# Second mixture of experts: raw float32 weights for few-token experts, splitting in an expert's own first tile, a ring of 21 raw pieces

## The chip, the cores and the metric

The kernel runs on one core of a Trainium2 chip. The metric is device microseconds of one execution. Three runs of the kernel before the change gave 1115.76, 1119.74 and 1121.19 us; their median is the time before.

The core's engines are TensorE (PE in the rows, its weight loads PEld), VectorE (DVE), ScalarE (ACT), GpSimd (POOL) and SyncE (SP). Each has its own instruction stream and takes it in order. SP issues nearly all plain DMAs here, POOL the indirect ones (gathers and scatters of rows by token number).

## The reference

Attention (4 x 8 heads, 576 positions, 64 wide, with rotary embedding) gives 2304 tokens of 512 numbers. A first mixture, in fact a dense gated layer with 1536 hidden columns, gives x. The change is in what follows:

```python
skip_score = x @ w_skip
do_compute = skip_score > 0
out = x.copy()
xc = x[do_compute]
e_idx = np.argmax(xc @ w_gate, axis=1)          # one of 8 experts
gate_w = softmax(xc @ w_gate)[its expert]
for e in range(8):
    h = np.maximum(xc[mask] @ w1[e], 0.0)       # 512 x 1024
    y[mask] = gate_w[mask, None] * (h @ w2[e])  # 1024 x 512
out[do_compute] = xc + y
```

With the inputs of the measurement the reference sends 299, 35, 55, 544, 28, 14, 322 and 1 tokens to experts 0 to 7.

## The kernel before

All matrix products are to be as exact as float32, but the fast operand type (float32r) isn't. So an operand a is split into a high part (a copy that ScalarE rounds to float32r) and a low part (a minus the high part, on VectorE or GpSimd), and a product is the sum of three: high x high, high x low, low x high.

**Order of the work.** Attention comes first (class `Attention`), then the first mixture (`Moe1`, chunks of 384 tokens, 12 steps f each), then the routing and the second mixture (`Moe2`). The code gives the order of each engine's instructions by hand; nothing is rescheduled. While the last chunk of the first mixture runs, `before(f)` loads and splits expert 0's weights into slots that are already free, then the first pieces of expert 1's. `first()` runs expert 0's first tile between the steps of the last chunk's routing: transposes and logits on PE, then `route` (L716 to L734, a chain of small VectorE operations), `place`, and the lists of the next tiles. Expert 0's first list is padded to 128 places there (`close_first`: before the last chunk it had 100 tokens), so that its count becomes 327.

**Experts and tiles.** `run` (L1259) takes expert after expert, in tiles of 128 tokens. Whether a tile exists is known only on the chip: `If` branches on every engine (L1291 for an expert's first tile, `more`, L1301 and L1327, for the later ones). A tile of more than 64 tokens goes through `ffn`: `up` (L1077, L1080: for each half of the 1024 columns 8 + 4 products of 512 columns), `turn` (L1134, transposes of h), `down` (L1150 to L1153: 24 products), `store` (L1158, L1159). A tile of at most 64 tokens (`few=True`) has the high and the low part of x side by side in one operand of 128 columns: 16 products up (L1094), a fold with the transpose (L1107), 16 products down (L1118).

**Weights before.** An expert has 8 raw pieces of 512 KB: 4 of w1, 4 of w2. `w_load` (L997) brings a piece into a ring of 7; `w_split` (L1015, L1017 high parts; L1020 low parts) splits it into one of two sets of slots, in turn for odd and even experts. An expert's first tile splits the next expert's weights (`work`, L1247): ScalarE, VectorE and GpSimd share that by the table `SPLITS`. Between the two halves of `turn`, `mid` transposes the next tiles' rows (`x_T`, L1063 to L1065), which POOL gathered (L1056). Each split piece's place in the ring is reloaded behind it in SP's stream.

**Lists.** After the routing, 8 lists of token numbers (L1043, 9 KB each, 12 bytes a place) are read from the table in DRAM, and VectorE limits the numbers (`numbers`, L1048) before POOL gathers the rows.

The lines on which the order rests:

```python
for e in range(E):
    if e == 0:
        self.more(0, n[0], ix[0], self.x01, self.x02, 1); continue
    ...
    with self.tc.If(n[e] > FEW) as cmp:                                   # L1291
        self.ffn(e, x0[e], self.work(e + 1, False), lambda: mid(False))
        self.more(e, n[e], ix[e], x1[e], x2, 1)
    with cmp.Else():
        self.ffn(e, x0[e], self.work(e + 1, True), lambda: mid(True), few=True)
```

Of the kernel before, what the change touches and what calls it, by code (L numbers as in the profile page):

```python
# [13 lines left out]
P = 128  # L14
# [8 lines left out]
class Attention:  # L23
    """Attention of all head pairs, one 128-row block of scores ("unit") after another; what
    a pair needs is prepared while the units before it run."""
# [45 lines left out]
    # the slots of it, from the pair's first unit  # L71
# [3 lines left out]
    # other slots for the first pair's, which all wait for, and the second's  # L75
# [47 lines left out]
    # the engines of RoPE and of the split: GpSimd (p), VectorE (v), ScalarE (a); of the first  # L123
    # pairs others
# [4 lines left out]
    # of the first pair's transposes and swaps, those that VectorE brings from PSUM  # L129
# [168 lines left out]
    def misc(self):  # L298
        """A bank for the slot's small transposes."""
# [42 lines left out]
    def sums(self, u):  # L342
        """1 / (row sums + 1e-9) of the pair."""
# [6 lines left out]
    def sums_out(self, u):  # L350
        """They leave as rows."""
# [13 lines left out]
    # a pair's thirds of halves, in the slots from LAG["pv"] after its first: early in a slot and late  # L365
# [67 lines left out]
class Weights:  # L433
    """Split weights live in slots of [128, 4, 512]; raw pieces of [128, 512] pass through a ring."""
# [14 lines left out]
    def slot(self, i, name):  # L449
        pool = self.early if i < self.nearly else self.late  # L450
        return pool.tile([P, 4, 512], F32R, tag=f"w{i}", name=name)

    def load(self, key, src, wide):
        """A piece in float32, or in float64 as pairs of words."""
# [5 lines left out]
    def narrow(self, key, hi, lo):  # L460
        """float64's words to float32: sign, exponent and fraction move into place; what is
# [953 lines left out]
```

## Time and profile before

| | us |
|---|---|
| median of three runs | 1119.74 |
| lowest, highest run | 1115.76, 1121.19 |
| span of the profiled execution, first to last instruction | 1110.7 |
| the same, from the first tile of expert 0 after the routing (862.5) to the end | 248.2 |

PE is busy for 987.0 us (89% of the span), VectorE 622.4, GpSimd 528.5, ScalarE 509.9. The mean granted TensorE clock is 0.964 of full speed. 121.2 MB are moved, 109 GB/s over the span. The profiled execution has no run time of its own beside its span; the span lies 9.0 us under the median of the runs.

How to read it: the busy shares are means over three stages with different limits. The page's 40 slices show PE at nine tenths or more through the first mixture, and holes in the last quarter only, which is where the changed code stands. What the change is worth is therefore read from a table of stretches of that quarter, from the waits of PE in it, and from the queue of DMAs.

### The profile page before, as it was taken

To read this page: it belongs to the slowest core of one execution; us is meant where nothing else is said; L and a number is where in the kernel's file an instruction comes from. 1 tells how busy PE (TensorE), PEld (TensorE's weight loads), DVE (VectorE), ACT (ScalarE), POOL (GpSimd) and SP (SyncE) were. 2 spreads that over 40 slices of the span, in tenths; PEclk is the share of its full clock that TensorE was granted. 3 is DMA by queue.
4 is the path that set the end of the run, shared out by engine and by line. 5 is a ranking of instruction groups with operands and counts; after the bars stand their busy time and mean duration, and the time that the engine had idled before them with its cause. 6 is when DMAs were issued, how large, how long until landed. Compare 5 with 4: busy or idle time off the path is not lost. (4 is left out here: it accounts for less than half of the span.)

```text
span 1110.7 us, 16633 instructions
## 1 busy us (share of the span) xinstructions
PE 987.0 (89%) x5883; PEld 834.7 (75%) x5883; DVE 622.4 (56%) x1006; ACT 509.9 (46%) x1093; POOL 528.5 (48%) x493
## 2 busy tenths in 40 slices
PE   5989889989997989899999999999998948996874
PEld 4766666666775878799999999999996736775763
DVE  6766776676774888863452432332546227615940
ACT  4777777776784333333432312322434226314510
POOL 6666678767821444452134152151345228514840
PEclk9999999999999999999999999999999968998896
DMA  5344455555423333332221212113245538704710
GB/s 160 101 117 107 121 153 132 140 148 127 124 78 129 114 114 103 108 86 85 58 71 56 60 29 71 44 29 98 73 125 166 160 99 270 236 31 141 250 46 3
DMA packets 81738, 121.20 MB, mean 109 GB/s; under 512 B 36645, under 2 KB 47541, under 8 KB 81600
## 3 DMA queue, kind: packets, MB, share of 16 engines
q1 hardware_dynamic: 77856, 110.02, 34.6%
q0 software_dynamic: 3744, 9.50, 2.7%
q8 instruction: 68, 1.11, 0.5%
q14 instruction: 70, 0.57, 0.2%
HBM read 88.78 MB, written 22.61 MB: 100 GB/s over the span
## 5 line engine op out<-in xcount | busy, mean ns | idle before, releaser
L614 POOL TENSOR_TENSOR hl<-h,hh 128x384 fp32r<-128x384 f32 x72 | 78.1, 1085 | 242.4 <-ACT hh L613 236.2
L252 DVE TENSOR_REDUCE nm<-S 128x1 f32<-128x576 f32 x144 | 108.5, 754 | 46.8 <-PE S L240 45.7
L260 ACT ACTIVATE P<-S,nm 128x576 f32<-128x576 f32 x144 | 107.0, 743 | 4.2 <-DVE nm L252 4.0
L1020 POOL TENSOR_TENSOR el<-we,eh 128x512 fp32r<-128x512 f32 (+1 forms) x55 | 85.0, 1571 | 42.4 <-ACT eh L1015 14.5
L613 ACT CAST hh<-h 128x384 fp32r<-128x384 f32 x72 | 37.0, 514 | 145.0 <-DVE h L612 145.0
L611 DVE TENSOR_TENSOR h<-g,h 128x384 f32<-128x384 f32 x72 | 40.0, 556 | 107.1 <-ACT h L610 107.1
L1020 DVE TENSOR_TENSOR el<-we,eh 128x512 fp32r<-128x512 f32 (+1 forms) x59 | 71.8, 1250 | 44.8 <-ACT eh L1015 38.6
L627 PE MATMUL Y<-ohi,hh 128*128 128x512 f32 x216 | 87.8, 407 | 5.4 <-ACT ohi L493 5.4
L270 PE MATMUL T<-ident,P 128*128 128x128 f32 x576 | 89.3, 278 | 0.0
L627 PE MATMUL Y<-ohi,hl 128*128 128x512 f32 x216 | 86.9, 402 | 1.4 <-POOL hl L614 1.3
L627 PE MATMUL Y<-olo,hh 128*128 128x512 f32 x216 | 86.0, 398 | 0.6 <-POOL olo L496 0.6
L319 PE MATMUL pv<-pt,rawv 128*64 128x384 f32 (+1 forms) x512 | 84.8, 432 | 1.5 <-ACT pt L285 1.4
L240 PE MATMUL S<-Ak,Aq 128*128 128x288 f32 x256 | 81.4, 333 | 1.5 <-ACT P L260 1.5
L604 PE MATMUL g<-xa,ghi 128*128 128x384 f32 x216 | 75.5, 350 | 7.1 <-DVE h L611 6.5
L240 PE MATMUL S<-Bk,Aq 128*128 128x288 f32 x256 | 73.1, 300 | 1.5 <-DMA Bk<-Ak 1.3
L610 ACT ACTIVATE h<-g 128x384 f32<-128x384 f32 x72 | 35.1, 487 | 85.4 <-PE g L606 81.6
L1015 ACT CAST eh<-we 128x512 fp32r<-128x512 f32 (+1 forms) x104 | 59.8, 649 | 30.9 <-DMA we<-in_moe_w_dram 16.6
L606 PE MATMUL g<-xa,glo 128*128 128x384 f32 x216 | 72.4, 335 | 0.0
L606 PE MATMUL v<-xa,vlo 128*128 128x384 f32 x216 | 72.2, 334 | 0.0
L604 PE MATMUL v<-xa,vhi 128*128 128x384 f32 x216 | 72.1, 334 | 0.0
L612 DVE TENSOR_TENSOR h<-v,h 128x384 f32<-128x384 f32 x72 | 40.2, 558 | 46.1 <-PE v L606 43.5
L270 PEld LDWEIGHTS T<-ident,P 128*128 128x128 f32 x576 | 63.5, 142 | 2.1 <-issue 1.2
(251 smaller groups left out, 2708.4 us busy)
## 6 DMA issues: line engine op xcount, KB each, us to landing
we<-in_moe_w_dram SPq DMA_DIRECT2D x64, 512.0 KB
xT<-x SPq DMA_DIRECT2D x32, 288.0 KB
x<-xT SPq DMA_DIRECT2D x24, 384.0 KB
Bk<-Ak SPq DMA_DIRECT2D x30, 288.0 KB
raw<-in_moe_w_gate_dram SPq DMA_DIRECT2D x12, 512.0 KB
raw<-in_moe_w_val_dram SPq DMA_DIRECT2D x12, 512.0 KB
raw<-in_moe_w_out_dram SPq DMA_DIRECT2D x12, 512.0 KB
rawk<-in_k_dram SPq DMA_DIRECT2D x16, 288.0 KB
```

Of the source, the lines that this page charges most:

```text
L240: nc.tensor.matmul(ps[:, c, :288], l, r[:, c * 288:(c + 1) * 288], start=(j == 0), stop=(j == len(ops) - 1))
L252: nc.vector.tensor_reduce(nm, st_u["S"], axis=AX.XY, op=ALU.max, negate=True)
L260: nc.scalar.activation(pt.rearrange("p (a b) -> p a b", a=2), st_u["S"], AF.Exp, bias=st_u["nm"], scale=1.0, accum_out=self.pairs[p]["l"][ ...
L270: nc.tensor.transpose(ps[:, kt * P:(kt + 1) * P], pt[:, kt * P:(kt + 1) * P], self.ident)
L319: nc.tensor.matmul(ps[a * D:a * D + D, :n], st["raw"]["v"][:, h, 2 * third + a], self.pt[:, 2 * third + a, c0:c0 + n], start=(third == 0), ...
L604: nc.tensor.matmul(ps[m], wh[:, kt, cols], xh, start=(kt == 0), stop=False)
L606: nc.tensor.matmul(ps[m], wl[:, kt, cols], xh, start=False, stop=(kt == KT - 1))
L612: nc.vector.tensor_tensor(h, ps["v"], h, op=ALU.mult)
L614: nc.gpsimd.tensor_tensor(hl, h, f32(hh), op=ALU.subtract)
L627: nc.tensor.matmul(self.acc[c][t], a[:, cols], b, start=(f == 0 and i == 0), stop=(f == FT - 1 and i == 2))
L1015: self.nc.scalar.copy(hi[:, cols], raw[:, cols])
L1020: eng.tensor_tensor(lo[:, cols], raw[:, cols], f32(hi[:, cols]), op=ALU.subtract)
```

## The change

- Experts with at most 64 tokens no longer use split weights. `raw_ffn` multiplies the unsplit float32 pieces by an unsplit float32 copy of the transposed rows (`xf`, written in `x_T` with one more ScalarE copy). Its products have 64 output rows; alternate ones go to the upper and the lower 64 rows of one PSUM bank, and a fold with `fold2` adds the two.
- Larger experts split their own weights, in their first tile, into one single set of slots (`homes`): high halves all on ScalarE, low halves all on VectorE (`half`). GpSimd splits nothing in this stage, and the next expert's weights are no longer touched (`work`, `SPLITS` are gone).
- Raw pieces stand in a ring of 21 (16 in the slots that the second set of split weights and the first mixture had, 4 in the old ring, 1 new). Experts 1 and 2 are loaded in `before` and `first`, 5 pieces of expert 3 at the start of `run`, the rest behind each expert, in SP's stream after its branch.
- The last tile of an expert, if it has at most 64 tokens, is found by arithmetic (`rest`): its list is read by a DMA of its own, at an address from a register, its numbers limited, its rows gathered. Of a larger expert these three stand ahead of the first tile, its transpose at that tile's end. The `Else` branches for few tokens in `more` go away.
- Expert 0's later tiles get a branch of their own; its second tile there transposes the third one's rows.

```diff
     def before(self, f):
-        if 4 <= f < 11:
-            for i in ((0,), (1,), (2, 3), (4,), (5, 6), (7,), (8, 9))[f - 4]:
+        if 4 <= f < 10:
+            for i in ((0,), (1,), (2, 3), (4,), (5, 6), (7,))[f - 4]:
                 self.w_splits(i, i + 1, "vv" if f > 8 else "vp")
+        if f in (8, 9):
+            self.raw_slots(2 * f - 16, 2 * f - 14)
+            for i in range(4):
+                self.w_load(1, 4 * f - 32 + i)
...
     def first(self):
+        self.raw_slots(4, 8)
+        for i in range(8):
+            self.w_load(2, i)
-        h0 = self.up(0, self.x00, 0, between={0: y_T[:2], 1: y_T[2:], 2: [(self.w_splits, 10, 12, "pp")], 3: lg[:1]})
+        h0 = self.up(0, self.x00, 0, between={0: y_T[:2], 1: y_T[2:], 3: lg[:1]})
-        self.w_splits(12, 14, "pp")
-        self.w_splits(14, 15, "vv")
-        self.w_splits(15, 16, "vv")
...
+    def half(self, e, i, k):
+        which, n = i // KT, i % KT // 2
+        hi, lo = (x[:, 2 * (i % 2) + k, :] for x in self.homes(which)[n])
+        raw = self.w.raw[e, i][:, k * 512:(k + 1) * 512]
+        self.nc.scalar.copy(hi, raw)
+        self.nc.vector.tensor_tensor(lo, raw, f32(hi), op=ALU.subtract)
...
+    def ffn(self, x, mid=None, few=False, split=None, end=None):
+        half(range(KT), 0)
+        half(range(KT), 1)
+        h0 = up(0, x, 0)
+        rows(range(0, 3))
+        h1 = up(0, x, 1)
+        turn(0, h0)
+        rows(range(3, 5))
         if mid:
             mid()
+        turn(1, h1)
+        rows(range(5, 8))
+        if end:
+            end()
+        down(0)
         store(x)
+    def raw_ffn(self, e, x, mid):
+        side = lambda ps, a: ps[a * FEW:(a + 1) * FEW]
+        for fh in range(2):
+            ps = self.bank("H", f"rH{fh}")
+            for kt in range(KT):
+                nc.tensor.matmul(side(ps, kt % 2), x["f"][:, kt * FEW:(kt + 1) * FEW],
+                                 self.w.raw[e, kt][:, fh * 512:(fh + 1) * 512],
+                                 start=(kt < 2), stop=(kt >= 2), skip_group_check=True)
+            nc.scalar.copy(h, ps)
+        mid()
+        for fh in range(2):
+            for i in range(4):
+                nc.tensor.matmul(ps[:, i * FEW:(i + 1) * FEW], hs[fh][:, i * P:(i + 1) * P], self.fold2, start=True, stop=True)
+            nc.scalar.activation(hT[:, fh * 4 * FEW:(fh + 1) * 4 * FEW], ps, AF.Relu)
+        for n in range(8):
+            nc.tensor.matmul(side(self.y, n % 2), hT[:, n * FEW:(n + 1) * FEW],
+                             self.w.raw[e, KT + n // 2][:, n % 2 * 512:(n % 2 + 1) * 512],
+                             start=(n < 2), stop=(n >= 6), skip_group_check=True)
+        self.few_store(x)
...
+    def rest(self, e, n):
+        at = ((n + (P - FEW - 1)) >> 7) << 7
+        ix = self.rows(self.table[bass.ds(at + e * NTOK, P)].rearrange("(t p) c -> p t c", p=P), [1], "rest")
+        return self.gather((self.rest_rows, self.xrest), ix, 0), at
...
     def run(self, n):
+        for i in range(RING - 16):
+            self.w_load(3, i)
         ix = [self.load_rows(tiles[e], [NI], str(e)) for e in range(E)]
+        nxt = 16 + RING - 16
         for e in range(E):
             if e == 0:
-                self.more(0, n[0], ix[0], self.x01, self.x02, 1)
+                with self.tc.If(n[0] > P + FEW) as cmp:
+                    self.ffn(self.x01, mid=lambda: (self.x_T(self.x02), self.x_T(self.x10, 1)))
+                    i0 = ix[0], self.numbers(ix[0], self.p1, "0")
+                    x3 = self.gather(self.xn[1], i0, 3)
+                    self.more(0, n[0], i0, self.x02, x3, 2)
+                with cmp.Else():
+                    self.x_T(self.x10, 1)
+                r, at = self.rest(0, n[0])
+                with self.tc.If(n[0] > at):
+                    self.x_T(r)
+                    self.ffn(r, few=True)
                 continue
...
             with self.tc.If(n[e] > FEW) as cmp:
+                r, at = self.rest(e, n[e])
                 x2 = self.gather(self.xn[0], ix[e], 2)
-                self.ffn(e, x0[e], self.work(e + 1, False), lambda: mid(False))
+                self.ffn(x0[e], lambda: (self.x_T(x1[e]), after()), split=e, end=lambda: self.x_T(r))
                 self.more(e, n[e], ix[e], x1[e], x2, 1)
+                with self.tc.If(n[e] > at):
+                    self.ffn(r, few=True)
             with cmp.Else():
-                self.ffn(e, x0[e], self.work(e + 1, True), lambda: mid(True), few=True)
+                self.raw_ffn(e, x0[e], after)
+            while nxt < 8 * (E - 1) and nxt - RING < 8 * e:
+                self.w_load(nxt // 8 + 1, nxt % 8)
+                nxt += 1
```

## Rows read from the trace of the kernel before

**Rows 1.** Stretches after the routing: length, busy us (instructions) by engine, clock, DMA.

```profile
core 0: us, PE busy (x) PEld busy (x) DVE busy (x) ACT busy (x) POOL busy (x), PEclk, DMA share, GB/s
862.50:890.40 27.90, 27.20 (x123) 22.07 (x122) 6.78 (x15) 5.79 (x11) 7.81 (x8) 0.94 0.57 149
890.40:905.65 15.25, 0.00 (x0) 0.00 (x1) 2.92 (x10) 1.14 (x2) 5.26 (x5) 0.64 0.42 123
905.65:918.20 12.55, 12.52 (x52) 10.17 (x52) 6.11 (x9) 7.34 (x14) 3.59 (x3) 0.76 0.30 86
...
919.90:936.40 16.50, 12.84 (x53) 10.23 (x54) 13.73 (x17) 9.20 (x17) 13.76 (x9) 0.79 0.85 277
936.40:998.90 62.50, 60.42 (x293) 49.70 (x291) 29.31 (x33) 20.50 (x39) 26.08 (x23) 1.00 0.47 154
998.90:1004.80 5.90, 0.02 (x1) 0.05 (x1) 2.99 (x4) 1.62 (x3) 2.36 (x2) 0.92 0.11 22
1004.80:1020.60 15.80, 12.91 (x52) 9.95 (x52) 6.16 (x9) 7.38 (x14) 4.69 (x5) 0.71 0.44 137
...
1022.80:1038.80 16.00, 12.25 (x52) 10.18 (x53) 13.12 (x17) 8.51 (x16) 13.19 (x9) 0.79 0.84 274
1038.80:1079.20 40.40, 38.48 (x185) 31.39 (x183) 26.55 (x26) 15.78 (x29) 25.34 (x19) 1.00 0.38 120
1079.20:1089.20 10.00, 0.01 (x1) 0.00 (x0) 0.75 (x1) 0.00 (x0) 1.01 (x1) 0.66 0.09 23
1089.20:1100.60 11.40, 11.26 (x48) 9.03 (x48) 0.85 (x2) 1.94 (x4) 0.00 (x0) 0.85 0.01 1
```

**Rows 2.** Lines that end a tile of many and of few tokens.

```profile
L1158 DVE SCALAR_TENSOR_TENSOR o<-Y,ix,rows x10: 739/751/751, 863.9 to 1079.2; 128x512 f32<-128x512 f32 x10
L1126 DVE SCALAR_TENSOR_TENSOR o<-o,ix,rows x6: 744/1058/1079, 922.5 to 1101.9; 64x512 f32<-64x512 f32 x6
```

**Rows 3.** PE's waits from 858 us on: total, times, longest.

```profile
PE H L1094 <- issue: 28.2, 3, 15.3
PE Y L1153 <- DVE pair L1137: 3.8, 2, 1.9
```

**Rows 4.** Branches of PE's sequencer at L1291: ns min/median/max, first and last start.

```profile
L1291 PEldq COMPARE_BRANCH  x7: 82/4342/7178, 898.3 to 1084.2; - x7
```

**Rows 5.** The last chunk's routing: timeline of DVE, POOL, PE; one wait of PE.

```profile
846.37 1.27 DVE L717 TENSOR_TENSOR rd<-lgs,rmx 128x24 f32<-128x24 f32 x1
851.22 0.17 DVE L723 TENSOR_TENSOR rge<-rge,rmx 128x24 f32<-128x24 f32 x1
...
841.34 9.94 POOL L1020 TENSOR_TENSOR el<-we,eh 128x512 fp32r<-128x512 f32 x8 [5.03 <-ACT eh L1015]
...
861.54 0.66 PE L1063 MATMUL xT<-ident,rows 128*128 128x128 f32 x4 [2.17 <-DMA rows<-x2d,gi]
...
PE rk L745 <- DVE roh L725: 3.2, 1, 3.2
```

**Rows 6.** PE between the two products of expert 1, timeline.

```profile
912.21 1.00 PE L1107 MATMUL hT<-fold,h 128*128 128x64 f32 x8
...
914.31 0.48 PE L1118 MATMUL Y<-eh,pair 128*128 128x512 f32 x1
914.62 0.39 PE L1118 MATMUL Y<-el,pair 128*128 128x512 f32 x1
914.85 0.40 PE L1118 MATMUL Y<-eh,pair 128*128 128x512 f32 x1
```

**Rows 7.** Attention's float32 products into 64-row halves, timeline of PE.

```profile
302.60 0.87 PE L319 MATMUL pv<-pt,rawv 128*64 128x384 f32 x4
303.40 0.44 PE L314 MATMUL pv<-pt,vt 128*128 128x384 f32 x1
...
305.50 0.87 PE L319 MATMUL pv<-pt,rawv 128*64 128x192 f32 x8
```

**Rows 8.** Low halves on VectorE, timeline; and the full tile by the chain.

```profile
927.82 1.89 DVE L1020 TENSOR_TENSOR el<-we,eh 128x512 fp32r<-128x512 f32 x3
...
976.70 1.86 PE H L1077 x8
...
989.28 3.65 PE H L1094 x16
```

**Rows 9.** SP's issues, VectorE's read of the first list, DMA rate per quarter us from 875.

```profile
875.46 1.40 SPq L997 DMA_DIRECT2D we<-in_moe_w_dram  x3
876.91 8.10 SPq L1043 DMA_DIRECT2D ix<-table  x8
...
883.28 0.17 DVE L1048 TENSOR_SCALAR gi<-ix 128x6 uint32<-128x6 int32 x1 [4.66 <-DMA ix<-table]
...
GB/s 0 0 0 0 0 0 33 0 82 16 164 205 262 377 401 385 361 360 410 401 377 393 401 418 410 401 309 122 125 323 317 269 102 32 18 10 21 21 14 18
```

More of the change, by code (lines that the diff above doesn't have):

```diff
@@ L979, in open @@
         self.p1 = ctx.enter_context(self.tc.tile_pool(name="e_1", bufs=1))
-        self.ring = ctx.enter_context(self.tc.tile_pool(name="e_r", bufs=3))
+        self.fold2 = self.p1.tile([P, FEW], F32, tag="fold2", name="fold2")
+        self.nc.vector.tensor_tensor(self.fold2, self.ident[:, :FEW], self.ident[:, FEW:], op=ALU.add)
+        self.raws += [self.w.ring.tile([P, F2], I32, tag="raw", name=f"wr{i}") for i in range(4)]
+        self.raws.append(self.p1.tile([P, F2], I32, tag="raw2", name="wr4"))
+        self.rest_rows = self.p1.tile([P, DM], F32, tag="rest_rows", name="rest_rows")
+        self.xf = [self.p1.tile([P, 4 * FEW], F32, tag=f"xf{i}", name=f"xf{i}") for i in range(2)]
+        self.xrest = self.p1.tile([P, 2 * DM], F32R, tag="xrest", name="xrest")
     def bank(self, kind, name):
@@ L1065, in x_T @@
         nc.vector.tensor_tensor(x["l"], ps, f32(x["h"]), op=ALU.subtract)
+        if few is not None:
+            x["f"] = self.xf[few]
+            nc.scalar.copy(x["f"].rearrange("p (k c) -> p k c", k=KT), ps.rearrange("p (k c) -> p k c", k=KT)[:, :, :FEW])
     def up(self, e, x, fh, work=(), between={}):
@@ L1160, in store @@
                                      bounds_check=NTOK - 1, oob_is_err=False)
-    def ffn(self, e, x, work=((), (), ()), mid=None, few=False):
+    def ffn(self, x, mid=None, few=False, split=None, end=None):
         up, turn, down, store = (getattr(self, "few_" * few + f) for f in ("up", "turn", "down", "store"))
-        hs = [up(e, x, fh, work[fh]) for fh in range(2)]
-        turn(0, hs[0])
+        half = (lambda ns, k: [self.half(split, i, k) for i in ns]) if split is not None else lambda ns, k: None
+        rows = (lambda ns: [self.half(split, KT + n // 2, n % 2) for n in ns]) if split is not None else lambda ns: None
+        if split is not None:
+            self.homes(0), self.homes(1)
+        half(range(KT), 0)
[5 more added lines that the diff above has]
+        rows(range(3, 5))
@@ L1262, in run @@
         tiles = [tiles[e, 0:NI * P].rearrange("(t p) c -> p t c", p=P) for e in range(E)]
-        self.raws = [self.w.ring.tile([P, F2], I32, tag="raw", name=f"we{i}") for i in range(4)]
-        self.raws += [self.ring.tile([P, F2], I32, tag="raw2", name=f"we{i}") for i in range(4, 7)]
-        for i in range(7):
-            self.w_load(2, i)
+        for i in range(RING - 16):
+            self.w_load(3, i)
         ix = [self.load_rows(tiles[e], [NI], str(e)) for e in range(E)]
         x0, x1 = [None, self.x10], [self.x01]
+        nxt = 16 + RING - 16
         for e in range(E):
             if e == 0:
-                self.more(0, n[0], ix[0], self.x01, self.x02, 1)
+                with self.tc.If(n[0] > P + FEW) as cmp:
[9 more added lines that the diff above has]
+                    self.ffn(r, few=True)
                 continue
@@ L1326, in more @@
-        with cmp.Else():
-            with tc.If(n > t * P) as few:
-                if e == 0 and t == 3:
-                    self.x_T(x)
-                self.ffn(e, x, few=True, mid=(lambda: self.x_T(self.x10)) if e == 0 and t == 1 else None)
-            if e == 0 and t == 1:
-                with few.Else():
-                    self.x_T(self.x10)
+                        y = self.gather(self.xn[0], self.rows(src, [1], "d"), 0)
+                        self.x_T(y)
+                        self.ffn(y)
```

108 lines of the change are left out of this document (43 added, 65 removed).

## The prediction

> **What bounds the kernel now.** The page's busy shares don't answer it: PE is at 89% of the span, but as a mean over three stages. I read a table of stretches of the last quarter first [rows 1]. There PE does all its work in stretches of which most are nearly full: expert 3 (936.40 to 998.90) has 60.4 us of PE in 62.5, expert 6 (1038.80 to 1079.20) 38.5 in 40.4. Two stretches have PE waiting within them, experts 2 and 5, with 12.8 and 12.3 us of PE in 16.5 and 16.0; VectorE and GpSimd are busy for 13 to 14 us there, so in these two the splitting is what ends last. Between stretches PE is empty: 15.3 us ahead of expert 1, 10.0 ahead of expert 7, 5.9 ahead of expert 4, and some 2 elsewhere. Ten tiles of many tokens and six of few ran [rows 2], which agrees with the counts of the reference, expert 0's padded to 327. The waits of PE [rows 3] name the large holes: three waits of few-token tiles with no releaser, 28.2 us, the longest 15.3. They are the branches: at L1291 alone PE's sequencer spends up to 7.2 us on one branch, 4.3 in the middle case [rows 4]. So this quarter is bound by PE, then by branches, then, in experts 2 and 5, by splitting. The change touches each.
>
> **The routing without splits, about -2 us.** In the last chunk's routing GpSimd splits expert 1's pieces, and VectorE's tiny operations beside it take long: a subtraction of 24 columns took 1.27 us at 846.37, within a GpSimd stretch of 9.9, another small one 0.17 at 851.22, just as that ends [rows 5]. Three such are slow by about 1.1 us each, and PE waits 3.2 us for that chain. Without these splits the wait goes: -3.3. Against it stands the gather of the second tile's rows, which costs PE 2.17 now [rows 5] and will meet the loads of experts 2 and 3: I give back 1.3. Bounds -3.3 and 0.
>
> **Expert 0's later tiles, +2 us.** The third tile's rows are transposed within the second tile, so PE waits there for a gather that it didn't need so early; a wait like the 2.17 is the nearest row. `fold2` on VectorE may stand behind what frees its place. Bounds 0 and +5.
>
> **Branches, -7 us.** Expert 0's chain loses the nested `Else` for few tokens: of the hole of 15.3 us I leave one branch of the long kind (7.2) and one small remainder, 8. A branch of 4.3 less is the one bound nearer to zero; the other is -11, one branch alone left [rows 4]. I put the end nearest zero at 0, since `rest` puts a new branch there. The other holes I keep at their size; a branch for each larger expert's rest comes instead of the ones that go, -3 to +4 in all.
>
> **Few-token experts from raw weights, about -12 us.** Before, such an expert has 16 products up, a middle, and 16 down; in expert 1 products follow each other by 0.23 us, and the middle, from 912.21 to 914.31, takes 2.1 [rows 6]. After, each half has 8 products, but in float32. The nearest row is attention's product into halves of 64 rows: four instructions of 384 columns, which are two products, take 0.80 us to the next product, and eight of 192 columns, four products, take as long as that row, 0.87 [rows 7]. So 768 columns cost 0.80, and 512 cost 0.53. One end is 0.58 (the row's own 0.87), the other 0.46, twice the 0.23. I take 0.53, since those rows too put alternate products into the two halves. Eight cost 4.25, an expert 4.25 + 2.1 + 4.25 = 10.6. Experts after a hole run at a lower clock for a while: expert 1's 16 products up took 6.5 us (905.65 to 912.21) at a mean grant of 0.76 in its stretch [rows 1], the same 16 products in expert 3 took 3.65 at full grant [rows 8], so 2.9 more. Against the stretches of rows 1: expert 1 13.5 for 12.55, +0.9; expert 2 10.6 for 16.5, -5.9; expert 4 13.5 for 15.8, -2.3; expert 5 10.6 for 16.0, -5.4; expert 7, last, with a grant of 0.85, 12.4 for 11.4, +1.0. Sum -11.7. The ends of the price give -17 and -8. The added ScalarE copy for `xf` and the folds stand beside PE and are at no cost; with that cover gone they cost 0.6 an expert.
>
> By the Trainium skill, "FP8 and Floating Point Precision", section "TensorE Precision Notes", a true float32 product takes four passes through the array. Four times 0.23 would be 0.92 for a product, and 80 x 0.39 = 31 us more in all; the rows of attention speak against it as a price of one product among two that run beside each other. That is a rival below.
>
> **Expert 3's first tile, +8.5 us.** Now its weights come split when it starts; a full tile takes 12.6 us (976.70 to 989.28) [rows 8]. After, VectorE must make 16 low halves within it. Three of 512 columns took 1.89, so 0.63 each and 10.1 in all [rows 8]; until the last one four more operations of 512 columns stand in its stream, some 0.75 each [rows 2]: 13.1. Behind the last low half come five products, 1.2 us, 2.2 at half the clock. I take 15 from the first low half to the tile's end.
>
> The first low half is not free at the start. `rest` stands ahead of the tile: SP issues a list read, and VectorE's `numbers` waits for it with all low halves behind it in VectorE's stream, and PE behind those. In SP's stream that read stands behind the eight reloads issued after expert 2, whose places come free only as expert 2's products read them: four after its second half up, four one by one in its down. Three to four loads will be in front. The price: the first list of before was issued at 876.91 behind three loads and read at 883.28, 6.4 us; the DMA rate then is about 390 GB/s, at which 512 KB take 1.35 us, so 2.3 remain for the read itself; one issue takes 1.0 [rows 9]. So 1.0 + 2.3 + 3.5 x 1.35 = 8.0, then 15: 23.0 for 12.6, +10.4. The second tile of before waited 1.9 us for VectorE [rows 3], then busy with the next expert's splits: that goes, -1.9. Bounds of the list: 3.3 with nothing in front, 14 with all eight; of the tile: +4 and +18.
>
> **Expert 6's first tile, +3.1 us.** Behind expert 5 there are only three reloads, of w1's places, free early; the list is there in time. What is left ahead of the halves is the branch and ScalarE's last copy: 2.0 (the small holes of rows 1, 1.7 and 2.2) and 0.6. Then 15: 17.6 for 12.6, +5.0, less the other wait of 1.9. Bounds +2 and +9.
>
> **How the numbers follow.** -2 + 2 - 7 - 11.7 + 8.5 + 3.1 = -7.1. The span of 1110.7 becomes 1103.6; the median stands 9.0 above the span, so 1119.74 - 7.1, about 1113. A measurement of this kernel can tell about 0.5%, 5.6 us, from no change. The forecast holds with 0.46, its own range 1105 to 1121: 0.24 faster by over 0.5%, 0.19 within, 0.03 slower.
>
> **Rivals.** One: the list comes early, because SP's queue is nearly empty by then. For it: the DMA share of these stretches stays under 0.85 in all and at 0.3 to 0.5 in most [rows 1]. Against: the reloads become possible just then. Expert 3's list at 3.3 for 8.0 and 1 to 3 saved elsewhere: 1106. Chance 0.14, all faster.
>
> Two: all eight reloads get their places only at expert 2's end. Then the list costs 1.0 + 2.3 + 8 x 1.35 = 14.1, +6.1, and expert 6's behind three, +3: 1122. It decides from a seventh load in front on. Chance 0.12, half within, half slower.
>
> Three: the branches don't shrink, since the new ones for the rest stand where the old `Else` stood: +7 ahead of expert 1 and up to +3 elsewhere, 1121 to 1123. For it: 4 to 7 us for one branch whatever it skips [rows 4]. Chance 0.13: 0.08 within, 0.05 slower.
>
> Four, on the other side: float32 products don't run beside each other in the two halves, so that each costs twice 0.53. 80 products (five experts) x 0.53 = +42, 1155. It decides from 0.62 on, where 80 x 0.09 eats the gain of 7.1, and makes the kernel slower by 0.5% from 0.69 on. Against it: attention's rows [rows 7] are of the same kind. For it: there it is two products at a time of fewer columns. With the four passes of the page above it would be 1144. Chance 0.10.
>
> Five: the change doesn't do what it says: a load in the ring that waits for a later expert's reader holds SP, and the raw experts wait for their own pieces. For it: eight pieces of 1.35 us are 10.8 an expert [rows 9], as long as a raw expert. Two such waits of 8 us: 1129. Chance 0.05, slower.
>
> Faster 0.24 + 0.14 = 0.38; within 0.19 + 0.06 + 0.08 = 0.33; slower 0.03 + 0.06 + 0.05 + 0.10 + 0.05 = 0.29. The range, 1100 to 1131, leaves out rival four and the far end of the first.
>
> **What would show it.** Right: attention's price again, raw products 0.5 to 0.55 us apart at full clock; experts 2 and 5 in 10 to 11 us; a hole of some 8 us ahead of expert 1; in expert 3's first tile PE waiting first on VectorE, VectorE on the list's DMA; expert 3 at about 71 us, expert 6 at about 43; the subtraction at L717 at about 0.2. Wrong: raw products 0.9 apart, a list that is there before the first high half, or GpSimd's gathers, not the list, as what PE waits for.

## The result, and the profile after

| | before | after |
|---|---|---|
| median (runs) | 1118.20 us (4) | 1130.09 us (4) |
| lowest, highest | 1115.76, 1121.19 | 1125.74, 1132.01 |
| span of the profiled execution | 1110.7 | 1129.4 |

The ratio is 1.0105, with a 95% interval of 1.0068 to 1.0141: the kernel became about 12 us slower. 1113 was forecast. The two profiled executions differ by 18.7 us, more than the medians do: after, each run lies 2.0 us above its span, so the profiled execution of before, at 1110.7, stands, by the same 2.0, for a short run of some 1113, not for the median. What makes its runs differ by that much was not found; below, the places are compared in the traces and the sums by the medians.

The table of stretches after, against [rows 1]. Columns: stretch and length, then busy us (instructions) of PE, PEld, DVE, ACT, POOL, the granted clock, DMA share, GB/s.

```profile
862.50:895.60 33.10, 29.24 (x125) 22.99 (x125) 7.79 (x18) 6.53 (x13) 7.83 (x8) 0.90 0.35 73
895.60:900.90 5.30, 0.00 (x0) 0.00 (x0) 1.23 (x9) 0.00 (x0) 1.98 (x2) 0.96 0.25 68
900.90:912.60 11.70, 11.09 (x52) 4.89 (x52) 0.69 (x1) 2.71 (x7) 3.79 (x4) 0.87 0.61 190
912.60:917.30 4.70, 0.00 (x0) 0.02 (x1) 1.43 (x2) 0.53 (x1) 1.65 (x2) 1.00 1.00 377
917.30:929.40 12.10, 11.39 (x52) 5.06 (x52) 0.69 (x1) 2.74 (x6) 1.21 (x2) 0.86 0.71 254
929.40:961.98 32.58, 18.30 (x69) 14.59 (x70) 14.59 (x24) 13.04 (x25) 5.15 (x5) 0.74 0.37 135
961.98:1009.40 47.42, 46.44 (x226) 38.37 (x225) 9.51 (x15) 9.98 (x19) 6.97 (x7) 1.00 0.19 59
1009.40:1015.30 5.90, 0.97 (x5) 0.50 (x4) 1.43 (x2) 0.58 (x1) 1.93 (x3) 0.82 0.91 342
1015.30:1027.80 12.50, 11.97 (x52) 5.67 (x52) 0.69 (x1) 2.71 (x6) 0.95 (x1) 0.81 0.67 236
1027.80:1031.70 3.90, 0.02 (x1) 0.05 (x1) 1.43 (x2) 0.58 (x1) 0.93 (x1) 0.81 1.05 408
1031.70:1047.80 16.10, 13.48 (x52) 5.24 (x52) 0.69 (x1) 2.72 (x6) 1.91 (x2) 0.73 0.56 207
1047.80:1074.70 26.90, 18.39 (x69) 14.66 (x70) 14.62 (x24) 13.03 (x25) 4.26 (x4) 0.75 0.20 51
1074.70:1099.80 25.10, 25.10 (x121) 20.48 (x119) 5.27 (x8) 5.36 (x10) 3.98 (x4) 1.00 0.13 43
1099.80:1108.10 8.30, 0.02 (x1) 0.01 (x1) 0.75 (x1) 0.00 (x0) 1.01 (x1) 0.63 0.09 26
1108.10:1119.20 11.10, 11.08 (x48) 5.17 (x48) 0.00 (x0) 1.95 (x4) 0.00 (x0) 0.82 0.01 1
```

Read it beside before: expert 0's later tiles 33.1 for 27.9; the hole ahead of expert 1 5.3 for 15.25; expert 1 11.7 for 12.55; a new hole of 4.7 for 1.7; expert 2 12.1 for 16.5; expert 3 32.6 + 47.4 = 80.0 for 62.5; a hole of 5.9 as before; expert 4 12.5 for 15.8, a hole of 3.9 for 2.2; expert 5 16.1 for 16.0; expert 6 26.9 + 25.1 = 52.0 for 40.4; a hole of 8.3 for 10.0; expert 7 11.1 for 11.4. The loss is in two rows, the first tiles of experts 3 and 6: 32.6 and 26.9 us, with 18 us of PE in each, for 12.6 of a full tile at full clock [rows 8].

Who waits for what there: PE's waits from 858 us on (total, times, longest), and VectorE's and SP's timelines at expert 3's start.

```profile
PE rH L1220 <- issue: 24.0, 5, 8.3
PE H L1104 <- DVE el L1043: 16.3, 2, 11.0
PE rH L1220 <- DMA out_dram<-o,ix: 5.6, 1, 5.6
...
924.26 0.69 DVE L1089 TENSOR_TENSOR xhl<-xT,xhl 128x512 fp32r<-128x512 f32 x1 [9.64 <-ACT xhl L1088]
930.78 0.74 DVE L1153 SCALAR_TENSOR_TENSOR o<-o,ix,rows 64x512 f32<-64x512 f32 x1
941.29 0.15 DVE L1071 TENSOR_SCALAR girest<-ixrest 128x1 uint32<-128x1 int32 x1 [9.77 <-DMA ixrest<-table]
941.43 4.95 DVE L1043 TENSOR_TENSOR el<-wr,eh 128x512 fp32r<-128x512 f32 x8
...
962.10 0.75 DVE L1185 SCALAR_TENSOR_TENSOR o<-Y,ix,rows 128x512 f32<-128x512 f32 x1 [3.23 <-PE Y L1180]
...
908.24 21.58 SPq L1006 DMA_DIRECT2D wr_s<-in_moe_w_dram  x16
933.07 0.17 SPq L1066 DMA_DIRECT2D ixrest<-table  x1
```

PE's largest wait for another engine is for the first low half (L1043), 11.0 us in expert 3. VectorE waits 9.8 of them for the list of the last tile (`girest` from `ixrest`); that list was issued by SP at 933.07, behind the reloads, and read at 941.29.

### The profile page after: what moved, and what is told of

It is laid out like the page before. It is cut to its first block, busy times and chain, and to the rows that moved or that the text cites. A ratio compares the mean times of both kernels' runs of the same rounds, so it can differ in the third digit from the quotient of the medians.

```text
span 1129.4 us, 16625 instructions
## 1 busy us (share of the span) xinstructions
PE 995.9 (88%) x5895; PEld 819.4 (73%) x5895; DVE 560.3 (50%) x967; ACT 482.7 (43%) x1047; POOL 453.0 (40%) x448
## 5 line engine op out<-in xcount | busy, mean ns | idle before, releaser
L612 DVE TENSOR_TENSOR h<-v,h 128x384 f32<-128x384 f32 x72 | 40.2, 558 | 47.4 <-PE v L606 44.9
L283 DVE COPY pt<-T 128x512 f32<-128x512 f32 x64 | 44.3, 692 | 32.0 <-PE T L270 30.6
L1220 PE MATMUL rH<-wr_s,xf 128*64 128x512 f32 x80 | 29.7, 882 | 29.6 <-issue 24.0
L240 PEld LDWEIGHTS S<-Ak,Aq 128*128 128x128 f32 x256 | 49.4, 193 | 6.5 <-issue 4.2
```

The lines of the kernel that those rows point to most:

```text
L240: nc.tensor.matmul(ps[:, c, :288], l, r[:, c * 288:(c + 1) * 288], start=(j == 0), stop=(j == len(ops) - 1))
L283: self.nc.vector.tensor_copy(self.pt[:, :, cols], self.units[u]["T"])
L612: nc.vector.tensor_tensor(h, ps["v"], h, op=ALU.mult)
```

## The experiments

In the table the places are measured alike for all kernels, from VectorE's stores: expert 0's later tiles (its first store to its third), experts 1 and 2 (on to expert 2's store), the first tiles of experts 3 and 6 (from the store before to their own), and the list of expert 3 (from expert 2's store to `girest`). The expectations count from PE's last product, 1.4 us ahead of that store. The ratio is against before, its interval in brackets. The kernels were not all timed together: the runs of before that go with them have medians from 1114.5 to 1118.2 us. So kernels are compared by their ratios, of which 0.001 is 1.1 us; their medians can differ by some us without cause.

| kernel | expert 0 | 1 and 2 | list of 3 | first tile 3 | first tile 6 | median, us | ratio |
|---|---|---|---|---|---|---|---|
| after | 31.6 | 35.5 | 10.5 | 31.3 | 25.6 | 1130.1 | 1.0105 (1.0068 to 1.0141) |
| x1_list_late | 32.7 | 36.2 | 12.8 | 25.5 | 25.8 | 1127.1 | 1.0094 (1.0063 to 1.0124) |
| x5_list_first | 31.5 | 34.1 | 0.7 | 18.7 | 18.6 | 1112.2 | 0.9957 (0.9928 to 0.9985) |
| x11_no_reload2 | 32.4 | 35.5 | 4.0 | 22.0 | 25.4 | 1124.3 | 1.0070 (1.0045 to 1.0095) |
| x9_mid_first | 30.9 | 38.8 | 7.5 | 28.2 | 22.8 | 1127.2 | 1.0122 (1.0053 to 1.0191) |
| x2_rows_first | 31.4 | 34.9 | 10.5 | 27.9 | 22.8 | 1125.6 | 1.0085 (1.0052 to 1.0117) |
| x3_fold2_late | 29.5 | 36.6 | 10.5 | 28.5 | 22.5 | 1128.2 | 1.0100 (1.0072 to 1.0129) |
| x7_list_rows | 29.4 | 34.0 | 0.7 | 18.1 | 18.1 | 1109.8 | 0.9935 (0.9914 to 0.9956) |
| x6_next_split | 29.6 | 40.9 | 0.7 | 17.8 | 15.3 | 1112.8 | 0.9961 (0.9937 to 0.9985) |
| x10_pool_lows | 29.0 | 34.1 | 0.7 | 18.9 | 22.4 | 1114.9 | 0.9981 (0.9958 to 1.0003) |
| x8_few_split | 31.7 | 39.7 | 4.0 | 24.3 | 24.9 | 1130.4 | 1.0117 (1.0054 to 1.0179) |
| x4_same_half | 31.3 | 40.3 | 5.7 | 26.5 | 23.2 | 1131.8 | one run |
| x12_one_half | 31.6 | 41.3 | 7.8 | 25.6 | 22.7 | 1139.6 | 1.0216 (1.0149 to 1.0283) |

Two lengths stand in the columns of first tiles where the order of the work is the same and the clock differs. From `girest`, just ahead of the first low half, to the store such a tile takes either 18 us (18.0 and 17.9 in x3_fold2_late) or 21 (20.8 and 20.9 in the changed kernel): PE comes back to full clock sooner or later after its idle time. What decides which, no run shows. The second part of expert 3's first tile, in the changed kernel and in x3_fold2_late (columns as in the table of stretches):

```profile
951.00:962.00 11.00, 8.99 (x41) 7.35 (x40) 6.19 (x10) 5.74 (x12) 0.00 (x0) 0.84 0.01 1
...
949.50:957.90 8.40, 6.39 (x32) 5.20 (x31) 5.95 (x10) 4.75 (x10) 0.00 (x0) 1.00 0.01 2
```

A difference of 2.8 in one of these columns therefore says nothing about an edit.

**The list.** Is it the price, and what is it late behind? The theory was the read behind eight reloads, the rival another wait in the same place. First the reader of the list was moved, then the read itself, then the loads.

```diff
 x1_list_late
-                r, at = self.rest(e, n[e])                  # read, numbers, gather
+                ixr, at = self.rest(e, n[e])                # the read alone
-                self.ffn(x0[e], lambda: (self.x_T(x1[e]), after()), ...
+                self.ffn(x0[e], lambda: (self.x_T(x1[e]), after(), rs.append(self.rest_in(ixr))), ...
 x5_list_first
+            if e + 1 < E:
+                ixr, nat[e + 1] = self.rest(e + 1, n[e + 1])
             while nxt < 8 * (E - 1) and nxt - RING < 8 * e:
 x11_no_reload2
-            while nxt < 8 * (E - 1) and nxt - RING < 8 * e:
+            while e != 2 and nxt < 8 * (E - 1) and nxt - RING < 8 * e:
 x9_mid_first (raw_ffn)
         hs = []
+        mid()
...
-        mid()
```

> Only edit to the changed kernel: VectorE's `numbers` on the list of an expert's last tile, and GpSimd's gather behind it, move from ahead of the first tile's halves into its middle (behind the transposes of the next rows). SP's read of the list stays where it is. Theory (the list read, behind eight reloads, holds all low halves): expert 3's first low half comes about 2 us after expert 2's last product instead of 12.1, its first tile takes 22 to 24 us instead of 32.7, expert 6's 22 to 23 instead of 27.0; the kernel is 12 to 14 us shorter, about 1117. Rival (VectorE would have to wait anyway, for ScalarE's high halves or for PE): the first tiles lose 2 us at most and the time stays at 1128 to 1130.

It took VectorE's wait away, and half of the gain came back as another wait: the gather of the last tile's rows now comes late, and PE waits for it in front of `down`. PE's timeline in x1_list_late:

```profile
933.75 0.76 PE L1104 MATMUL H<-el,xhl 128*128 128x512 f32 x1 [1.01 <-DVE el L1043]
949.48 1.09 PE L1087 MATMUL xT<-ident,rest_rows 128*128 128x128 f32 x4 [6.80 <-DMA rest_rows<-x2d,girest]
```

Expert 3's first tile lost 5.8 us, expert 6's nothing, where 9 to 11 and 4 to 5 were expected; the ratio hardly moved. So the late list has two users, and moving one shows the other.

> Only edit to the changed kernel: SP issues the list read of the next expert's last tile ahead of the reloads behind an expert instead of behind them (numbers and gather stay at the head of the next expert's first tile). Theory (the eight loads in front of the list are the price): the first low half of expert 3 comes about 2 us after expert 2's last product instead of 12.1, of expert 6 about 2 instead of 6.4; first tiles about 22.5 each; 14 us shorter, about 1116. Rival (the list's own wait for the scatters of earlier tiles, or VectorE's wait for something else, is the price): less than 4 us, 1126 or more.

The list is there before VectorE asks (0.7 us after the store), the first tiles come to 18.7 and 18.6 us, 12.6 and 7.0 less, and the ratio falls by 0.0148, some 16.5 us: below before. The theory holds, by a little more than the 14 expected. Of the two tiles' gain 9.8 and 4.1 are the list (to `girest`); the rest is the clock, back sooner in both (18.1 and 17.9 from `girest`). This one edit undoes the whole loss. It does more than change places in SP's stream, though: the list has two places in turn, and it is read behind every expert, outside the branch. The next run takes away the loads alone.

> Only edit to the changed kernel: the eight reloads behind expert 2 are issued behind expert 3 with the others; the list read stays where it is. Theory (those eight loads, 10.8 us, are what expert 3's list waits for): the first low half of expert 3 comes 2 to 4 us after expert 2's last product instead of 12.1, its first tile takes 22 to 23 us instead of 32.7; experts 4 and 5 may wait a few us for their pieces; 5 to 9 us shorter. Rival (SP waits for the scatter of an earlier tile and issues the list late, whatever is loaded): the wait stays above 8 us.

With no loads in front the first low half still came 5.6 us after expert 2's last product: over the theory's 2 to 4, under the rival's 8, so there is something of both. SP's and GpSimd's timelines in x11_no_reload2 show what is left:

```profile
933.92 0.93 POOL L1154 DMA_INDIRECT out_dram<-o,ix  x1 [12.37 <-DVE o L1153]
...
935.09 0.35 SPq L1066 DMA_DIRECT2D ixrest<-table  x1
```

The list's read is issued just behind the scatter of expert 2's rows, and SP's waits name that scatter. So of expert 3's wait in the changed kernel, 12.1 us from expert 2's last product (929.35) to the first low half, 3.7 go to the scatter (list issued at 933.07) and 8.2 to the loads (933.07 to 941.29), of which 1.8 is the read by itself (935.09 to 936.93 here). The loads alone are thus worth 6.4.

> Only edit to the changed kernel: a raw few-token expert transposes the next expert's rows ahead of its products up instead of between up and down. In the trace of the changed kernel the first reload behind expert 2 is issued at 925.10, just after VectorE's low part of that transpose (924.26, 0.69 us), though piece 0 of expert 2 was read by 922.7 at the latest. Theory (SP's reloads wait for that VectorE operation, not for their own places): the reloads start up to 4 us earlier, fewer of them stand in front of the list, expert 3's first low half comes 8 to 9 us after expert 2's last product instead of 12.1; 3 to 5 us shorter in all. Rival (the reloads wait for the end of up or for the down): the wait stays at 11 to 12 us, no change.

The first reload behind expert 2 now starts 6.6 us before that expert's down ends (925.27 of 931.9) instead of 4.3 (925.10 of 929.35), the four of w1 together, those of w2 one by one, as I had forecast it for the change; the low half comes 9.0 us after the last product. So in the changed kernel SP waited for the transpose's VectorE operation. The time didn't follow (the ratio is no lower): expert 1's transpose, now in front, waits 9.7 us for a gather, and what expert 3 gained experts 1 and 2 lost (3.1 and 3.3).

**The tile's own length.**

```diff
 x2_rows_first
+        rows(range(0, 8))
         h0 = up(0, x, 0)
-        rows(range(0, 3))
 x6_next_split (with x5 and x3)
-            split=e
+            split=e if e not in (3, 6) else None
-                self.raw_ffn(e, x0[e], after)
+                self.raw_ffn(e, x0[e], after, split=e + 1 if e in (2, 5) else None)
 x10_pool_lows (with x5, x3 and x2)
+        eng = self.nc.gpsimd if which and k else self.nc.vector
-        self.nc.vector.tensor_tensor(lo, raw, f32(hi), op=ALU.subtract)
+        eng.tensor_tensor(lo, raw, f32(hi), op=ALU.subtract)
```

> Only edit to the changed kernel: all eight halves of w2 come ahead of the first tile's products in the streams of ScalarE and VectorE, instead of 3 behind the first half up, 2 behind the first `turn`, 3 behind the second. Theory (after the list the tile takes 20.6 us instead of my 15 because ScalarE's high halves stand behind its evacuation of h, which waits for PE, so VectorE waits 4.4 us for them): expert 3's first tile goes from 32.7 to about 29, expert 6's from 27.0 to about 23.5, the kernel to about 1123. Rival (those waits of VectorE are covered; PE's half clock and the order of `turn` behind the low halves set the end): no change, 1129 to 1131, or the tile grows by 1 to 2.

The numbers came, 3.4 and 2.8 us less, but they don't bear the theory out. From `girest` expert 3's tile takes 17.3 and expert 6's 18.0, and x3_fold2_late, which leaves this order as it is, has 18.0 and 17.9. VectorE's waits for ScalarE are gone, and the tile is 0.7 and 0 shorter: they were covered, as the rival has it. The rest is the clock. The run also shows what a first tile is bound by. VectorE's last low halves, and PE's two parts of the tile:

```profile
945.62 3.69 DVE L1043 TENSOR_TENSOR el<-wr_s,eh 128x512 fp32r<-128x512 f32 x6
...
939.40:948.00 8.60, 7.71 (x29) 6.29 (x30) 8.59 (x15) 0.95 (x2) 2.30 (x2) 0.74 0.24 61
948.00:956.70 8.70, 7.44 (x41) 6.22 (x40) 4.39 (x8) 3.16 (x7) 0.00 (x0) 1.00 0.01 3
```

The low halves are done at 949.31, 7.4 us before the store at 956.75, and PE is busy for 15.2 of the 17.3 us: 12.6 of a full tile, and the start at a lower clock. So it is PE that ends last here, not the low halves.

> Edits to the changed kernel: the list read ahead of the reloads, `fold2` later, and all halves of w2 ahead of the first tile's products (as in x2_rows_first). It computes for any token counts. Theory (the three costs add up, each in its own place): first tiles of 15.5 to 16 us instead of 18.7, expert 0's later tiles 2 us shorter: about 1105. Rival (with the list early the low halves are the bound, and w2's halves ahead of `turn` delay PE's products): first tiles of 18.5 or more, 1110 to 1112.

The rival was nearly right on the tiles: they take 18.1, 0.6 less than in x5_list_first. What came on top is `fold2` (expert 0's tiles 2.1 less). This kernel beats both others: 0.65% under before, 1.7% under the changed one by the two ratios.

> Edits to the changed kernel: the list read ahead of the reloads (as in x5_list_first), `fold2` made later (as in x3_fold2_late), and the halves of experts 3 and 6 are made beside the few-token experts 2 and 5 ahead of them, where VectorE and ScalarE have little to do, instead of in their own first tiles. This fixed choice fits the token counts of the measured inputs alone. Theory (what is left of the loss sits in splitting inside the own first tile): the first tiles of experts 3 and 6 go from 18.7 us in x5_list_first to 13 to 14, experts 2 and 5 grow by at most 2 each; 6 to 10 us under x5_list_first less 2 for `fold2`: about 1100 to 1104. Rival (PE's clock after the few-token experts and the gathers hold the first tiles): 16 to 18 us each, about 1108 to 1110.

Neither. Expert 2 alone takes 21.1 us for 15.3 in x7_list_rows: the halves stand in ScalarE's stream between the copies of the raw products, PE waits up to 2.4 us for one, and its down then takes 6.4 at a granted clock of 0.57 instead of 3.65 at 1.00. Expert 3's tile came only to 17.8, because PE now waits 3.9 us for the gather of the last tile's rows. Splitting early moved the cost into the expert ahead.

> Edits to the changed kernel: list read ahead of the reloads, `fold2` later, w2's halves ahead of the products, as in x7_list_rows, and four of the eight low halves of w2 on GpSimd. It computes for any token counts. Theory (VectorE's 16 low halves, 10 us, with `turn` behind them, bound the first tile of 18.1 us in x7_list_rows): first tiles of 15 to 16 us, the kernel at 1104 to 1106. Rival (GpSimd's gathers stand ahead of its halves and it takes 1.3 us for one, and VectorE is slower beside it): 18 us or more, 1110 to 1114.

The rival, and worse: expert 6's tile takes 22.4. VectorE's and GpSimd's timelines in x10_pool_lows:

```profile
1039.40 8.97 DVE L1043 TENSOR_TENSOR el<-wr_s,eh 128x512 fp32r<-128x512 f32 x6
1041.91 5.86 DVE L1043 TENSOR_TENSOR el<-wr_s,eh 128x512 fp32r<-128x512 f32 x1
...
1042.23 4.98 POOL L1043 TENSOR_TENSOR el<-wr_s,eh 128x512 fp32r<-128x512 f32 x4
```

The first line is six low halves of VectorE, the second is one of them. Five take 0.63 each, as ever [rows 8], also beside GpSimd's gathers (1038.29 to 1042.21); the one that began just ahead of GpSimd's four subtractions takes 5.86 and ends 0.6 after them. What GpSimd takes over, VectorE loses. In expert 3's tile VectorE was through (935.3) before GpSimd subtracted (from 935.52); with four low halves less on VectorE that tile still took 18.2 from `girest`, for 17.4 in x7_list_rows. So VectorE's low halves, the theory's bound, do not bound it.

**`fold2`.**

```diff
-        self.nc.vector.tensor_tensor(self.fold2, self.ident[:, :FEW], self.ident[:, FEW:], op=ALU.add)   # in open
+                self.nc.vector.tensor_tensor(self.fold2, ...)                                             # in run, e == 1
```

> Only edit to the changed kernel: VectorE makes `fold2` just ahead of expert 1's numbers instead of when the stage opens, where it waits 10.2 us for the scatters into the table. Theory (that wait holds VectorE's low part of h, and PE behind it): expert 0's second and third tile go from 32.4 to 28, PE's wait of 2.3 us there goes, the kernel to about 1125.5. Rival (PE waits for the gathers or runs at half clock anyway): 1129 to 1130.

Expert 0's tiles lost 2.1 us, where 4.4 was expected; the ratio fell by 0.0005, which the intervals don't tell from nothing. The rest is another wait. VectorE's wait for `fold2` in the changed kernel (rows leave out the 2), and a wait of PE in x3_fold2_late:

```profile
875.41 0.23 DVE L982 TENSOR_TENSOR fold<-ident 128x64 f32<-128x64 f32 x1 [10.20 <-DMA table<-rrow,rposu]
...
PE Y L1176 <- ACT pair L1162: 2.4, 1, 2.4
```

The second tile now transposes two tiles' rows in its middle, and ScalarE's copy of h's own transpose stands behind theirs.

**Raw products.**

```diff
 x8_few_split
-                self.raw_ffn(e, x0[e], after)
+                self.ffn(x0[e], after, few=True, split=e)
 x4_same_half
-            side(ps, kt % 2) ... side(self.y, n % 2)
+            side(ps, kt // 2) ... side(self.y, n // 4)
 x12_one_half
-            side(ps, kt % 2) ... self.fold2 ... side(self.y, n % 2)
+            ps[:FEW] ... self.ident[:FEW, :FEW] ... self.y[:FEW]
```

> Only edit to the changed kernel: the five few-token experts go back to split weights, which they split in their own tile, into the same single set of slots as the large ones. It tells what the raw float32 products are worth in this order of the work. Theory (raw products take VectorE's low halves off the path): the few-token experts take 16 to 18 us each instead of 11 to 16, the kernel 20 to 30 us longer, 1150 to 1160. Rival (the few-token experts are bound by branches and PE's clock, not by splitting): under 5 us longer.

The rival's number came, but not its reason. Experts 1 and 2 took 4.2 us more, 4 and 5 some 3.5, expert 7 0.6. But expert 3's list came 6.5 earlier after expert 2, and its first tile lost 7.0: the last reload was issued by 934.01, ahead of expert 2's store at 935.49, and the list, read from 937.60 to 939.45, had no loads to wait for. What the raw products save is given back at the next list.

> Only edit to the changed kernel: in the raw float32 products, two successive ones go to the same 64 rows of the bank up, four in the down, instead of to alternate halves. The sums are the same. Theory (alternate halves run beside each other, as I read attention's rows): products 0.45 us apart become about 0.9 apart where neighbours share a half, 60 to 70 of 80 products dearer by 0.45, about 1155 to 1165. Rival (0.45 is the price of a product of 64 rows by itself): nothing changes, 1126 to 1132.

> Only edit to the changed kernel: all raw float32 products of an expert go to the upper 64 rows of the bank, none to the lower ones; so there is nothing to fold, h is transposed with 64 rows of the identity, and the store needs no sum of two halves. In x4_same_half four neighbours in one half made the eight products down 5.42 us instead of 3.65 at a granted clock of 1.00, but neighbours in pairs cost nothing. Theory (products into different halves run beside each other, also a few places ahead of their turn): without any to the other half every one takes two times 0.43, eight take about 6.9 at full clock, some 6.5 more for an expert less 1 to 2 for the fold and the store: 80 products x 0.43 - 8 = 25 to 30 us longer, about 1156. Rival (what x4_same_half showed was something of its own order, not the halves): eight still take 3.7 to 5.4, the kernel 1120 to 1138.

The eight products of expert 1's down, all at a granted clock of 1.00, in the order of the changed kernel, x4_same_half, x12_one_half:

```profile
908.84 3.65 PE L1235 MATMUL Y<-wr_s,rhT 128*64 128x512 f32 x16 [0.48 <-ACT rhT L1232]
...
909.77 5.42 PE L1235 MATMUL Y<-wr_s,rhT 128*64 128x512 f32 x16 [0.49 <-ACT rhT L1232]
...
913.46 7.08 PE L1234 MATMUL Y<-wr_s,rhT 128*64 128x512 f32 x16 [0.27 <-ACT rhT L1231]
```

Alternating halves 3.65, four neighbours in one half 5.42, all in one half 7.08. So products into different halves do run beside each other, and the price of one alone is 7.08/8 = 0.88; the theory holds. How far ahead PE takes them, x4_same_half shows, where a product is two of PE's instructions. L1235 in three stretches of that down (length, PE, PEld, clock, DMA share, GB/s):

```profile
909.75:911.50 1.75, 1.73 (x4) 0.60 (x5) 1.00 0.66 121
911.50:913.25 1.75, 1.75 (x9) 0.72 (x8) 1.00 1.02 394
913.25:915.20 1.95, 1.94 (x6) 0.41 (x3) 1.00 1.06 395
```

First four instructions, 0.43 apart, then about eight in the same time, then four and what runs over: the second half's products begin when two of the first half's four are still to come. So pairs of neighbours cost nothing (3.67 up).

As for the time, both experiments missed: 1131.8 and 1139.6 for 1155 to 1165 and 1156. In x4_same_half only the down grew, by 1.8 an expert. In x12_one_half some 30 us were added on PE, and some 12 arrived by the ratio (1.0216 for 1.0105). PE's timeline there shows one place where the rest went, beside the branch ahead of expert 2 in x12_one_half and in the changed kernel (ns least, middle, most; start):

```profile
920.92 7.05 PE L1219 MATMUL rH<-wr_s,xf 128*64 128x512 f32 x16 [0.38 <-issue]
...
L1360 PEldq COMPARE_BRANCH  x1: 6551/6551/6551, 914.2 to 914.2; - x1
...
L1358 PEldq COMPARE_BRANCH  x1: 7492/7492/7492, 909.5 to 909.5; - x1
```

The hole ahead of expert 2, 4.8 us in the changed kernel, is 0.4. The branch takes 6.6 us for 7.5, but PE has products until 920.54 for 912.49. Both first tiles are shorter too, 25.6 for 31.3 and 22.7 for 25.6; 2.7 of that is expert 3's list, and 3.0 and 2.8 are the clock.

## Why the prediction was wrong, by its own steps

**The routing, -2.** Half right. Its VectorE operations are short now (L717 0.18 for 1.27 [rows 5]), but PE waits 3.4 us for the second tile's gather instead of 2.17, and expert 0's first store comes at 863.70 for 863.87: zero.

**Expert 0's later tiles, +2.** +5.2 (33.1 for 27.9), just beyond the end of +5. `fold2` waited 10.2 us for the table's scatters and held VectorE's stream, which x3_fold2_late prices at 2.1. The other part that I named, the third tile's gather, costs 0.5 there; I had left out ScalarE's copies of two more transposes, 2.4.

**Branches, -7.** -7.0 in all, but by luck, from two misses. The hole ahead of expert 1 shrank by 10.0, within the bounds; what is left of it, 5.3, is put down to the scatter of expert 0's rows (5.6 in PE's waits), not to a long branch as I had it. And raw experts 2 and 5 start behind larger holes (4.7 for 1.7, 3.9 for 2.2): +4.7, a little over the +4; that expert 7's shrank by 1.7 brings it back to +3. Rival three is out.

**Raw experts, -11.7.** -0.9, -4.4, -3.3, +0.1, -0.3: -8.8, within -17 and -8. The price of a product was mis-sized to the good, 0.46 for 0.53 (3.65 us for eight), and halves side by side is what the experiments bear out. Expert 5 failed: for 10.6 it still takes 16.1, with 2.0 us of idle PE in the middle of its up that no other engine explains, and a granted clock of 0.73; the others make up for it, so that the sum fits is in part luck. Rival four is out: it is what x12_one_half makes of the kernel. Rival five is out too: none of PE's waits names a load of weights. By the Trainium skill, "FP8 and Floating Point Precision", section "TensorE Precision Notes", a true float32 product takes four passes, which with this kernel's 0.23 would be 0.92, an estimate; x12_one_half agrees with 0.88. By the Trainium skill, "TensorEngine Tiling (Array Packing)", section "Key Properties", different tiles of the array can run products in parallel; two at a time would make 0.46 of that, an estimate, and the trace agrees with 3.65/8 = 0.46.

**Expert 3's first tile, +8.5.** This is the step that failed: +17.5, just inside its bound of +18. It has two terms, the list (8.0) and the tile behind it (15), and both were too small. For the list the way was right. Of 8.0 for it 12.1 came, by rival two's arithmetic nearly (14.1): all eight loads were in front, because SP held the first until VectorE's part of the transpose, and the list waited 3.7 us for the scatter of expert 2, which I hadn't seen; its own read was shorter (1.8 for 2.3).

Of 15 for the tile 20.7 came (941.4 to 962.1), 18 where the clock came back sooner: the larger of the two misses, and here the path was wrong. I had added up VectorE's operations, 13.1, and put five products behind the last low half. But PE ends last: x2_rows_first has the low halves done 7.4 us before the store, x10_pool_lows takes four of them from VectorE, and in neither is the tile shorter than 17.3. PE's own work, 12.6 at full clock, takes 17.8 here, at a granted clock of 0.64 up to 951 us and 0.84 from there. Behind the wait for the list I should have priced it at the lower clock, as I had done for the raw experts. And PE waits within the tile. Its timeline shows what stands ahead of the down, which I had let run beside the last low halves:

```profile
950.82 1.04 PE L1087 MATMUL xT<-ident,rows 128*128 128x128 f32 x8
951.70 0.60 PE L1161 MATMUL hT<-ident,h 128*128 128x128 f32 x4
954.30 0.66 PE L1087 MATMUL xT<-ident,rest_rows 128*128 128x128 f32 x4 [2.01 <-DVE xhl L1089]
954.72 0.48 PE L1177 MATMUL Y<-eh,pair 128*128 128x512 f32 x1
```

The transposes of the last tile's rows are first in PE's stream and wait 2.0 us for VectorE, whose subtraction (L1089) reads an earlier transpose out of the bank; the whole down, 5.6 us at full clock (x5_list_first), 7.2 here, comes behind them. The change's `end` had stood in the diff; I left it out of the sum. What another place for it would give, no run shows.

**Expert 6's first tile, +3.1.** +11.6, beyond its bound of +9. I took the list as in time since only three loads are in front. It isn't the loads: the list waits for the scatter of expert 5's rows. SP's wait in that stretch, its read of the list, and VectorE's reader of it:

```profile
SPq L1066 <- DMA out_dram<-o,ix: 5.4, 1, 5.4
...
1051.82 0.36 SPq L1066 DMA_DIRECT2D ixrest<-table  x1
...
1053.86 0.15 DVE L1071 TENSOR_SCALAR girest<-ixrest 128x1 uint32<-128x1 int32 x1 [3.98 <-DMA ixrest<-table]
```

The first low half comes at 1054.06, 6.4 us after expert 5's last product instead of 2.6. For the list the failing step is not a size: I looked at the queue of loads and not at what the read itself waits for. The tile then took 20.7 for 15, by the same step as in expert 3, and that is the larger part.

**The sum.** -7.1 was forecast; +18.7 came by the traces, +11.9 by the medians. Of the 25.8 between forecast and traces the two first tiles are 17.5 (9.0 and 8.5), the raw experts 2.9, the holes ahead of experts 2 and 5 4.7, expert 0 3.2, the routing 2; the hole ahead of expert 1 gives back 3 and that ahead of expert 7 1.7, and the edges of the stretches are the last 0.2. And I took the 9.0 us between span and median for a constant, though it was mostly one short execution. The measured 1130.1 lies inside 1100 to 1131, but at the end that rivals had put there; the forecast's own range, 1105 to 1121, missed it, and so did its direction. x5_list_first, with 1112.2, comes out where I had put the change, but by coincidence: it has none of the wait for the list, for which I had allowed 8.0, and a longer tile, 18 for 15.

## What to carry to other kernels

Where a small read decides when an engine may start, look at everything in front of it: the loads in its queue and the scatter that its issuing engine waits for; then issue it ahead of both, which here gave some 16.5 us. And before one engine's work is summed up as a tile's length, add up the others too, TensorE at the clock that it will be granted: VectorE's 13 us looked like the bound, while TensorE had 15 to 18 us of work and waited 2 more for a bank.

Time that is taken from one engine counts only as far as the next wait follows it. Here 4 us saved on few-token experts only let the same list be waited for longer, and 30 us added on PE became some 12.

## What the runs showed of the hardware

- Float32 products of 512 columns and 64 output rows: 0.46 us each when they alternate between the halves of the rows, 0.88 when all go to one, 0.68 with four neighbours in one (eight in 3.65, 7.08, 5.42, at a granted clock of 1.00). Pairs of neighbours cost nothing (3.67): in x4_same_half PE began the other half's products two products ahead of their turn.
- VectorE's low halves of 128x512 take 0.63 us each, also beside GpSimd's gathers, but one that met four subtractions of GpSimd took 5.86, until they were over (x10_pool_lows). The small operations of the routing went from up to 1.27 [rows 5] to 0.18 without GpSimd's subtractions beside them.
- A branch on PE's sequencer takes up to 7.5 us (L1358 in the changed kernel: 70, 4345, 7492 ns least, middle, most), but it costs only as far as PE has run out of work: 4.8 us of hole before expert 2 became 0.4 in x12_one_half, where the branch still took 6.6 and the products queued ahead of it 7.1.
